# Spectral mixer with MLP, forward and backward on one core: half-row w2-gradient stores on ScalarE's queue, three half rows moved forward, an own tile for x1's gradient

## The chip, the core and the metric

The kernel runs on one core of a Trainium2 chip, in one launch. A core has five engines with an instruction stream each: TensorE (PE, matrix products), VectorE (DVE), ScalarE (ACT), GpSimd (POOL) and SyncE (SP), which here issues loads and stores only. They meet through semaphores. Matrix products land in PSUM, from where DVE or ACT copy them to on-chip memory (SBUF); DMA transfers move data between SBUF and HBM. The metric is the time of one execution in microseconds of device time, the median of several runs.

## The reference

A block with two branches, forward and then the whole backward pass, in bf16 with S = 2048 tokens, D = 1024 channels, F = 3584 hidden channels:

```python
def _A_ref(x, w_r, w_i):          # spectral mixer
    X = rfft2(x, axes=(-2, -1)) * (w_r + 1j * w_i)     # weights 2048 x 513
    return irfft2(X, s=(S, D), axes=(-2, -1)).astype(bfloat16)

def _B_ref(x, w1, b1, w2, b2):    # channel MLP
    y = _layernorm(x)
    h = _gelu(einsum('bsd,df->bsf', y, w1) + b1)       # tanh form
    return einsum('bsf,fd->bsd', h, w2) + b2

mod = (_silu(c) @ w_mod).reshape(c.shape[0], 6, 1, -1)
sa, ca, ga, sb, cb, gb = ...
x = x + ga * _A_ref(_layernorm(x) * (1 + ca) + sa, w_r, w_i)
x = x + gb * _B_ref(_layernorm(x) * (1 + cb) + sb, w1, b1, w2, b2)
```

Outputs are the block's result and the gradients of x, w_r, w_i, w1, b1, w2, b2, c and w_mod. Out of these, this case touches the gradient of w2 (3584 x 1024, `out_6`: h transposed times the gradient at the MLP's output), that of x (`out_1`), and, by their place in the order, those of the spectral weights (`out_2`, `out_3`), of w1 (`out_4`) and of w_mod (`out_9`).

## The kernel before

Work is tiled by P = 128 partitions; a PSUM tile holds 128 x 512 float32 (KH = 512). The forward pass and the MLP's backward come first. The last third of the time, from about 964 us on, runs two things side by side on PE: the backward of the spectral mixer, which is a chain with many hand-overs between engines, and a stock of plain matrix products that depend on nothing in that chain and are dealt out between its steps.

**The stock** is the generator `pieces` (line 1226). It yields first the w2 gradient in half rows: row fc (0 to 27, 128 rows of w2 each) and half h (512 columns) are one product of 16 matmuls of 128x512 (`gw2_product`, 1088, with `gw2_mm`, 1074), which accumulate in a PSUM tile with the tag f (four buffers); `gw2_out` (1078) copies it to SBUF and stores it. The two last rows' four products are interleaved, by token chunks. Then come 56 products of the w1 gradient (line 1266), 16 matmuls each. h comes in by transposing loads (`hh_load`, 1228), and the gradient at the hidden layer by transposing loads too (`gw1_load`, line 1217, tiles gzh), all on SP's queue. `fill(n)` (1277) takes n products.

**The chain** is `spectral_core` (from line 465) in its backward form. It runs eight pairs of frequency blocks: `pair` (495) takes the forward DFT along one axis (matmuls of line 505 into pcs, copied to the tile cs at lines 647 and 650), multiplies on DVE by the weights (tiles Pt, qa, qb, R, all through `tt`, line 173), and makes the gradients of the spectral weights in pf, stored by SP (551) and, by index, by POOL (552). `pair_load` (486) loads weights (490, 491) and the forward's spectrum d_P (493) for the next pair. After each pair `beside_bwd` (1302) takes four products of the stock, with steps of the w_mod gradient between them (`gmod_ring`, 981: load of a strip of w_mod at 986, DVE at 997 and 999, store on POOL at 1000). The inverse DFT `s_inv` (matmuls of line 565 into pv, copied to V by line 647) is done for two classes, CE and SE, ahead of pair 6, and for CO and SO after pair 7. Its pv tiles and half of the pcs and po tiles have the PSUM tag s with two buffers.

Then come four chunks of 512 tokens: matmuls of line 630 into po, copied to ct at 635, and `consume_bwd` (1184), the backward of the layer norm on DVE and ACT, which loads x again (`load_tok`, 128 and 131), adds x1's gradient (`d_gx1`, loaded at 1202 over the normed x) and stores the gradient of x. Between them `fill` takes 6, 6, 8 and 8 products and twice 2 ("norm quarters" are these chunks). After the chunks three more rows of the w_mod gradient follow, with eight products behind each, and the rest of the stock.

**What sets the order.** Each engine runs its own instructions in the order of the program that the scheduler lays down; `high_priority()` lets an instruction go ahead of others that are ready, and `issue_after` ties one to another. A `nc.any` operation is placed by the scheduler on the engine that it thinks free: this goes for the copies of lines 647 (`act_copy`, 646), 635, 1082 and 1270. A DMA from SP or ScalarE takes the next of eight completion semaphores, and waits until the transfer that had this semaphore before has landed; POOL's DMAs have eight of their own. Before the change, ScalarE issues no DMA in this part.

## Time and profile before

| | |
|---|---|
| three runs | 1459.1, 1463.76, 1466.73 us (median 1463.76) |
| the profiled execution | 1459.13 us, of which the span of its instructions 1457.3 |
| granted TensorE clock, mean | 0.992 |
| ACT's waits for a store of the w2 gradient (line 1082), 1000 to 1250 us | 12.6 us, 5 times |
| DVE's waits for the load of x1's gradient (line 173 after 1202) | 3.4 us, 2 times |
| share of the DMA engines, 1080 to 1160 / 1240 to 1360 us | 0.98 / 0.67 to 0.72 |
| last product of the stock ends | 1449.36 us |

In the stretches of 40 us from 1080 on, PE is busy this much (columns: stretch, length, then busy time and instructions of PE, PE's weight loads, DVE, ACT and POOL; then the clock granted to TensorE, the DMA share and GB/s):

```profile
1080.00:1120.00 40.00, 39.94 (x209) 20.22 (x207) 28.51 (x39) 13.22 (x22) 18.03 (x22) 1.00 0.98 249
1120.00:1160.00 40.00, 37.76 (x188) 18.28 (x189) 29.00 (x42) 16.29 (x28) 19.43 (x22) 1.00 0.98 252
1160.00:1200.00 40.00, 38.22 (x188) 18.16 (x187) 26.57 (x38) 14.00 (x25) 17.73 (x21) 1.00 0.85 226
1200.00:1240.00 40.00, 38.88 (x207) 19.43 (x206) 31.95 (x46) 20.00 (x27) 6.93 (x11) 1.00 0.82 223
1240.00:1280.00 40.00, 36.75 (x198) 18.58 (x198) 35.44 (x49) 17.86 (x23) 10.32 (x12) 1.00 0.72 196
1280.00:1320.00 40.00, 39.98 (x207) 19.24 (x205) 34.10 (x45) 17.69 (x23) 11.28 (x16) 1.00 0.69 198
```

How to read it: PE is the engine with the most work in every stretch, and from 1280 us on it never waits; it falls short of 40 us only between 1120 and 1280. That is where pairs 5 to 7, the inverse DFTs and the first chunks lie, and every edit of the change acts there or ahead of it.

### The profile page before, as it was taken

Reading aid. Unit: us, or ns where it says so; the run is one execution under the profiler, and the core shown is the slowest. Engines: PE = TensorE matmul, PEld = TensorE weight load, DVE = VectorE, ACT = ScalarE, POOL = GpSimd, SP = SyncE. Lnnn points to the kernel's source line nnn. Section 1 sums busy time; section 2 is a strip of 40 time slices with the busy share of each in tenths; the row PEclk is TensorE's granted clock in tenths of the full one; section 3 lists DMA queues with packets and bytes.
Section 4 is the critical chain, followed back from the end, with each engine's and each line's share of the span. In section 5 each row is a group of like instructions: output and inputs, shape, how many; then the busy total and the mean of one; then the engine's idle time right before and its main releaser. Section 6 shows DMA issues by size and latency. Waiting matters only on the chain. (4 is left out here: it accounts for less than half of the span.)

```text
span 1457.3 us, 18411 instructions
## 1 busy us (share of the span) xinstructions
PE 1396.5 (96%) x6835; PEld 649.0 (45%) x6835; DVE 1058.4 (73%) x1483; ACT 752.2 (52%) x1065; POOL 366.1 (25%) x441
## 2 busy tenths in 40 slices
PE   5889999999999999999999999999999999999997
PEld 2434545444444444444444444344444445444443
DVE  5884786898799787887520889898467678898650
ACT  4675555857887766665305574342622434344211
POOL 6520451211112122122211011021245441222432
PEclk8999999999999999999999999999999999999999
DMA  9962473899887877697998275297699987766991
GB/s 333 286 214 70 142 235 115 270 255 337 257 203 278 259 250 233 201 264 241 277 297 245 74 271 185 107 270 176 181 217 254 254 233 213 194 191 180 297 279 65
DMA packets 358367, 324.28 MB, mean 223 GB/s; under 512 B 209386, under 2 KB 301056, under 8 KB 358022
## 3 DMA queue, kind: packets, MB, share of 16 engines
q1 hardware_dynamic: 324166, 207.71, 52.7%
q0 software_dynamic: 34112, 115.41, 22.6%
q8 instruction: 53, 0.87, 0.2%
q14 instruction: 36, 0.29, 0.1%
HBM read 162.06 MB, written 111.20 MB: 188 GB/s over the span
## 5 line engine op out<-in xcount | busy, mean ns | idle before, releaser
L684 PE MATMUL pp<-gBoT,wt 128*128 128x512 bf16 x896 | 197.9, 380 | 4.5 <-DMA wt<-in_B_w_dram 2.6
L950 PE MATMUL pg<-w1T,gzr 128*128 128x512 bf16 x896 | 197.1, 381 | 0.2 <-ACT gn3b L961 0.2
L1266 PE MATMUL gw1acc<-gzh,n3n 128*128 128x512 bf16 x896 | 195.4, 379 | 1.3 <-DMA gzh<-d_gz 1.3
L684 PEld LDWEIGHTS <-wt 128*128 128x128 bf16 x896 | 87.7, 98 | 109.4 <-issue 4.2
L950 PEld LDWEIGHTS <-gzr 128*128 128x128 bf16 x896 | 87.3, 98 | 108.7 <-issue 6.6
L802 PEld LDWEIGHTS <-w 128*128 128x128 bf16 x896 | 87.3, 98 | 108.8 <-issue 4.7
L1266 PEld LDWEIGHTS <-n3n 128*128 128x128 bf16 x896 | 87.4, 98 | 106.1 <-issue 2.7
L802 PE MATMUL pz<-n3Tb,w 128*128 128x512 bf16 x448 | 99.2, 379 | 1.6 <-DVE w2sD L875 1.4
L802 PE MATMUL pz<-n3Ta,w 128*128 128x512 bf16 x448 | 98.7, 379 | 1.1 <-ACT gt L805 1.1
L1075 PE MATMUL gw2acc<-gB,hhsA 128*128 128x512 bf16 x448 | 98.5, 379 | 1.0 <-DMA hhsA<-d_hh 1.0
L853 PEld LDWEIGHTS <-hhA 128*128 128x128 bf16 x608 | 59.0, 98 | 71.7 <-issue 1.4
L805 ACT ACTIVATE gt<-pz,b_col 128x512 bf16<-128x512 f32 x112 | 72.5, 684 | 34.2 <-PE pz L802 32.8
L1270 ACT CAST gwo<-gw1acc 128x512 bf16<-128x512 f32 x50 | 29.1, 583 | 113.6 <-PE gw1acc L1266 99.0
L173 DVE TENSOR_TENSOR gt<-gt,gt 128x2048 bf16<-128x2048 bf16 x56 | 68.3, 1223 | 22.4 <-ACT gt L813 21.2
L1082 ACT CAST gwo<-gw2acc 128x512 bf16<-128x512 f32 x46 | 26.7, 583 | 109.9 <-PE gw2acc L1075 75.6
L811 ACT ACTIVATE gt<-gt 128x2048 bf16<-128x2048 bf16 x28 | 53.5, 1910 | 55.7 <-DVE gt L173 55.7
L173 DVE TENSOR_TENSOR ct<-ct 128x2048 bf16<-128x2048 bf16 x64 | 75.9, 1218 | 1.8 <-DMA d_n<-ct 1.1
L1075 PEld LDWEIGHTS <-hhsA 128*128 128x128 bf16 x448 | 43.6, 98 | 53.0 <-DMA hhsA<-d_hh 1.7
L997 DVE CUSTOM_DVE_ANT_0 otl<-otl 128x1024 bf16<-128x1024 bf16 x24 | 29.1, 1223 | 49.9 <-DMA otl<-in_w_mod_dram 44.2
L807 ACT ACTIVATE gt<-gt 128x2048 bf16<-128x2048 bf16 x28 | 53.4, 1908 | 5.4 <-DVE hhC L173 2.5
L813 ACT ACTIVATE gt<-gt 128x2048 bf16<-128x2048 bf16 x28 | 53.5, 1909 | 0.5
L1271 POOL DMA_DIRECT2D out_dram<-gwo x56 | 30.6, 548 | 85.6 <-ACT gwo L1270 53.4
(325 smaller groups left out, 2531.5 us busy)
## 6 DMA issues: line engine op xcount, KB each, us to landing
gzr<-d_gz SPq DMA_DIRECT2D x28, 512.0 KB
wblk<-in_w_mod_dram SPq DMA_DIRECT2D x12, 1024.0 KB
out_dram<-otl POOLq DMA_DIRECT2D x48, 256.0 KB
out_dram<-gwo POOLq DMA_DIRECT2D x96, 128.0 KB
d_ph<-pho POOLq DMA_DIRECT2D x21, 512.0 KB
d_hh<-hhA POOLq DMA_DIRECT2D x19, 512.0 KB
w2sD<-in_B_w_dram SPq DMA_DIRECT2D x14, 512.0 KB
hhC<-d_ph SPq DMA_DIRECT2D x14, 512.0 KB
```

The source lines that it names most:

```text
L173: return nc.vector.tensor_tensor(out=out, in0=a, in1=b, op=op)
L684: last_pe[0] = nc.tensor.matmul(pp[:], lhsT=wt[:, fg % 2, cch, k * P:(k + 1) * P], rhs=gBoT[j][:, cch, :], start=(cch == 0), stop=(cch == ...
L802: last_pe[0] = nc.tensor.matmul(pz[:], lhsT=w1s[g][:, cch, k * P:(k + 1) * P], rhs=n3T[:, cch, :], start=(cch == 0), stop=(cch == NDC - 1))
L805: nc.scalar.activation(out=zb[:, k, :], in_=pz[:], func=ACT.Identity, bias=b1_col[:, fc:fc + 1], scale=1.0)
L807: nc.scalar.activation(out=av, in_=zb, func=ACT.Square)
L811: nc.scalar.activation(out=sg, in_=bv, func=ACT.Sigmoid, scale=2.0 * GK)
L813: nc.scalar.activation(out=bv, in_=bv, func=ACT.Sigmoid, scale=-2.0 * GK)
L853: last_pe[0] = nc.tensor.matmul(pbs[i][:], lhsT=hh[:, k, i * P:(i + 1) * P], rhs=wp[:, k, :], start=False, stop=(g == 6 and k == 3))
L950: last_pg[0] = nc.tensor.matmul(pgs[i][:], lhsT=gzs[b, g][:, k, i * P:(i + 1) * P], rhs=w1Ts[g][:, k, h * KH:(h + 1) * KH], start=(g == 0 ...
L1075: nc.tensor.matmul(acc[:], lhsT=hh_of(fc)[:, t, :], rhs=gBs[t // 4][:, t % 4, h * KH:(h + 1) * KH], start=(t == 0), stop=(t == NT - 1))
L1266: nc.tensor.matmul(acc[:], lhsT=n3ns[t // 4][:, t % 4, cch * P:(cch + 1) * P], rhs=gz2[t // 8][:, t % 8, :], start=(t == 0), stop=(t == NT ...
L1271: nc.gpsimd.dma_start(out=out_4[cch * P:(cch + 1) * P, fg * 512:(fg + 1) * 512], in_=ob)
```

## The change

It has three parts.

1. `gw2_out`: for rows 8 to 27, the PSUM copy stands on ScalarE always, and the half row is stored by ScalarE, at high priority, and not by POOL.
2. `consume_bwd`: x1's gradient gets a tile of its own, gx (four rows of D per partition, tag smb, which smB2 held until the SO inverse), and its load is issued right behind that of x. The addition reads gx.
3. The stock: one product more behind pair 7, 7 and not 6 in the first two chunks; behind each of the last three w_mod rows 7 and not 8.

```diff
     def gw2_out(acc, fc, h):
...
         with tc.high_priority():
-            nc.any.tensor_copy(out=row[:, half], in_=acc[:])
-        if fc >= 8:
-            nc.gpsimd.dma_start(out=out_6[fc * P:(fc + 1) * P, half], in_=row[:, half])
-        elif h == 1:
+            (nc.any.tensor_copy if fc < 8 else nc.scalar.copy)(out=row[:, half], in_=acc[:])
+            if fc >= 8:
+                nc.scalar.dma_start(out=out_6[fc * P:(fc + 1) * P, half], in_=row[:, half])
+        if fc < 8 and h == 1:
             nc.gpsimd.dma_start(out=out_6[fc * P:(fc + 1) * P, :], in_=row)
...
-    accCA = []
+    accCA, gxt = [], []
...
             accCA.append(ps_s("accCA"))
+            gxt.append(reg.tile([P, 4, D], BF16, name="gx", tag="smb"))
...
         load_tok(n1, A_x, i)
+        nc.sync.dma_start(out=gxt[0][:], in_=chunk_rows(d_gx1, i))
         with tc.issue_after(last_po[0].ins):
             norm_act(n1, n1, 0, i)
...
-        nc.sync.dma_start(out=n1, in_=chunk_rows(d_gx1, i))
-        tt(o4, o4, n1, ALU.add)
+        tt(o4, o4, gxt[0][:], ALU.add)
         store_tok(out_1, o4, i)
-        fill((6, 6, 8, 8)[i])
+        fill((7, 7, 8, 8)[i])
...
+        if n == 7:
+            fill(1)
...
         gmod_row(r, w1g["ins"])
-        fill(8)
+        fill(7)
```

## The prediction

> **What bounds the kernel now.** I read the page's busy times, then the waits of TensorE (PE) in the stretch that the change touches (960 us to the end), then the timelines of PE, VectorE (DVE), ScalarE (ACT) and SyncE (SP) around the places where the edits land.

> ```profile
> PE 1396.5 (96%) x6835; PEld 649.0 (45%) x6835; DVE 1058.4 (73%) x1483; ACT 752.2 (52%) x1065; POOL 366.1 (25%) x441
> ```

> PE is busy 96% of the span: the end is set by the sum of its matmuls plus the moments when it waits. Its waits from 960 us on (engine, line, what it waited for: total, times, longest):

> ```profile
> PE po L630 <- ACT ct L635: 2.0, 1, 2.0
> PE pv L565 <- DVE R L173: 1.8, 1, 1.8
> PE gw2acc L1075 <- DMA otl<-d_hh: 1.3, 1, 1.3
> PE gw1acc L1266 <- DMA gzh<-d_gz: 1.3, 1, 1.3
> PE po L630 <- DVE ct L635: 1.1, 1, 1.1
> PE gw2acc L1075 <- DMA hhsA<-d_hh: 1.0, 1, 1.0
> ```

> Six waits, 2.0 + 1.8 + 1.3 + 1.3 + 1.1 + 1.0 = 8.4 us (rounded rows taken from the timeline). That is everything that any change of order can win here: 0.57% of 1459.13. What it can lose has no such bound.

> **The change part by part.** It takes no matmul away and adds none, so the sum is that of PE's waits, old against new. I read the new ones from the order of the changed kernel's instructions and the semaphores they wait for, and their times from rows of before.

> *1. The copy that moves to DVE.* Line 1082's PSUM copies of rows 8 and later are pinned to ScalarE. Line 647's copies (of pv, in the inverse DFT of class CE, just before pair 6) are still free for the scheduler to place. Before, all sixteen before pair 6 stand on ScalarE; in the changed order the first one stands on DVE, behind all of pair 5's arithmetic and two steps of the w_mod gradient (lines 997 and 999, twice). Class CE's pv tiles take turns in two PSUM buffers, so PE's third pv group waits for that copy.

> ```profile
> 1144.89 14.01 PE L565 MATMUL pv<-smi,R 128*128 128x512 bf16 x64
> ```
> ```profile
> 1146.01 0.59 ACT L647 CAST V<-pv 128x512 bf16<-128x512 f32 x1
> ```
> ```profile
> 1143.93 1.28 DVE L173 TENSOR_TENSOR Pt<-cs01b 128x1028 bf16<-128x1028 bf16 x2
> ...
> 1152.48 1.30 DVE L173 TENSOR_TENSOR pf<-qb 128x1026 bf16<-128x1026 bf16 x2
> 1155.63 1.23 DVE L997 CUSTOM_DVE_ANT_0 otl<-otl 128x1024 bf16<-128x1024 bf16 x1 [1.85 <-DMA otl<-in_w_mod_dram]
> ...
> 1159.93 0.49 DVE L999 TENSOR_SCALAR otl<-otl,u_rt 128x1024 bf16<-128x1024 bf16 x1
> ```

> Columns: start, time, engine, line, operation; in brackets the idle time before and what ended it. PE starts the first pv at 1144.89; a group of four matmuls is 14.01 / 16 = 0.87 us, so the third is due at 1146.6. DVE comes to the copy only after 1159.93 + 0.4 = 1160.3, and ends it at about 1161.0 (0.6 us, the ACT row, for want of one on DVE here). PE waits 1161.0 - 1146.6 = 14.4 us. Bounds: without the two waits for w_mod loads (1.85 + 1.27 us) DVE would be there 3.1 us sooner, 11.3; with one of the loads as late as the next one (which cost DVE 7.21 us in place of 1.27), 20.3. I take 14.4, since the loads are the same. What is queued behind the copy on DVE is the w_mod step before pair 6, which waited 7.21 us for its load anyway; behind PE's wait stand the rest of the inverse, pair 6's matmuls and everything after. DVE's pair 6 started at 1169.29 on copies that were there at 1162.0; these come 14.4 later, at 1176.4, so DVE loses only about 7 us of the 14.4 and has caught up with PE by 7.

> *2. ScalarE's stores wait in ScalarE's own order.* All DMAs of SP and ScalarE share eight completion semaphores in rotation, and each waits until the previous holder of its semaphore has landed. Before, SP alone used them. Now 40 half-row stores on ScalarE wait for whatever load of SP came eight DMAs before, and every copy behind them on ScalarE waits too. In pairs 0 to 5 the holders are loads of d_P (493), w_mod (986) and the stores of 551; the copies of pcs queued behind have room of 2.6 to 8 us before DVE wants them (DVE's pair cycle is 16.8 us, PE's 15.6), and gw2acc has four PSUM buffers: I cost them at 0; without that cover it would be the length of each late load, up to 4 us a pair. The last one is bare: the product that is added after pair 7 stores its half row just ahead of seven of CO's copies, and its semaphore's last holder is the third n3n load.

> ```profile
> 1199.71 0.42 SPq L1251 DMA_DIRECT2D n3n<-d_n  x1
> ...
> 1239.43 0.53 SPq L1202 DMA_DIRECT2D xt<-d_gx  x1
> ```

> SP issues it after DVE's pair 7, 6.7 us later than now: 1206.4; a load of that size (d_gx, 1 MB, issued at 1239.43, used at 1246.03) lands 6.6 us on, 1213.0; issue and copy end at 1214.2. PE starts CO's inverse at 1189.86 (its three matmuls ahead of the 1.78 us wait) + 14.4 + 3.46 (the added product of 16 matmuls: half of 1216.03 to 1222.94, the time PE took for two of them at line 1075) = 1207.7 and needs the second buffer back for the fourth group, 2.6 later: 1210.3. Wait 3.9 us; from 0 (the load lands in 2.7 us) to 8. [...]

> *3. One product before CO's inverse* (3.46 us of PE work, moved from the end): it covers the 1.78 us wait for DVE's R, and part 1's shift covers it too: -1.8.

> *4. Two quarters with 7 for 6.* In chunk 1 the extra product brings the gw1 products earlier relative to their first transposed loads. The first product needs the third of SP's transposes:

> ```profile
> 1226.59 12.75 SPq L1217 DMA_TRANSPOSE gzh<-d_gz  x3
> ```
> ```profile
> 1243.34 1.02 PE L1266 MATMUL gw1acc<-gzh,n3n 128*128 128x512 bf16 x4 [1.25 <-DMA gzh<-d_gz]
> ```

> It landed at 1243.3, 20.4 us after the four interleaved last products began (1222.94). In the changed order PE comes to it after these four (13.8 us) and one stretch of other matmuls, 15.6 us after their start: a wait of 4.8 us, from 2 to 6, in place of the 1.1 (line 630, which is now elsewhere) and the 1.3.

> *5. x1's gradient in its own tile.* The load goes out ahead of the norm's arithmetic, and DVE's add no longer waits for it (3.4 us in two waits now). DVE is then through a chunk in some 34.5 us, PE's chunk with nine products (31.1), its po matmuls (3.5) and sums (0.6) is 35.2: PE's 1.98 us wait for line 635 goes, all but 0.5. The tile takes the place of smB2, whose last reader is the SO inverse; the load is queued on SP before the last transposes of hh, and 1 MB there is inside part 4's bound.

> *6. What stays.* The waits for hh (0.96 + 1.34 us) stand on the same order of SP's loads: 2.3. At the end three products fewer run beside and after the w_mod rows; DVE's last step of those (line 977, at 1422.07) ends 26 us before the last product (1449.36), so 26 - 3 x 3.46 = 15.7 us of room is left and nothing waits; the 8 us after the last product stay. POOL loses 40 issues of 0.55 us; at 18 us busy in 40 it was no one's bound: 0.

> Sum of PE's waits after: 2.3 + 14.4 + 3.9 + 4.8 + 0.5 = 25.9; before 8.4: +17.5 us. On the profiled execution (1459.13; span 1457.3 and 1.83 around it) 1476.6. That execution is 4.6 us below the median of the runs (1463.76; 1459.1 to 1466.73), so about 1481 for a median.

> **The rivals.**
> - *DVE comes in time.* DVE's pair 5 had its inputs on chip (the copies of pcs) at 1132; it started at 1143.93 because of a 5.71 us wait for a load in the w_mod step ahead of it and of loads in the pairs before. If taking the 40 stores off POOL's queue loosens that chain of stores and loads, DVE can be up to 11.9 us earlier. The stall of part 1 needs 13.3 us of DVE work after that start (14.4 less 1.1 us of waits that go), so it is gone if pair 5 starts by 1133.3; part 2's load is then earlier as well. PE's waits would be 2.3 + 4.8 + 0.5 = 7.6, 0.8 less than before: 1463; with the transposes in time too, 1458. For it: POOL's share of busy time. Against: line 552's indirect stores on POOL wait for line 551's landing, not for line 1084's issues.
> - *The copy is no stall, but the stores' waits are.* The first V copy is done in time, and ScalarE still blocks before CO's inverse: PE would be at the fourth group at 1195.9, the load, issued at 1199.71, lands between 4.4 (a w_mod load, issued at 1154.25, used at 1158.66) and 6.6 us later, plus 1 us: 9.2 to 11.4 us. With parts 4 to 6, 10 + 7.6 - 8.4 = +9: 1473. Against it: the order, which has the copy behind pair 5.
> - *ScalarE blocks in the pairs as well.* The covers of part 2 are used up once DVE and PE have come level; two or three late loads of 4 us on PE's path: +8 to +12 on top, 1491. For it: the DMA share is 0.98 from 1080 to 1160, so loads are late there. Against it: DVE, the slower one, sets the pace in the pairs.

> **How the numbers follow.** My forecast 0.74, DVE in time 0.08, copy no stall 0.10, blocks in the pairs 0.08. The forecast's own range is 1474 to 1489 (part 1 from 11.3 to 20, part 2 from 0 to 8, part 4 from 2 to 6, not all at one end). The range 1467 to 1491 reaches into the second rival and up to the third and leaves out the first. About 0.5% (7.3 us, the spread of the three runs) can be told from no change: faster 0.03 (of the first rival's), same 0.11 (the rest of it and the half of the second that falls under +7.3), slower 0.86.

> **What would show it.** Right: PE's largest wait in the new profile is pv of line 565 for a DVE copy of line 647, of 11 to 20 us, 1.7 us after CE's inverse starts, with DVE in lines 997 and 999 just before it; a wait of pv for ACT before CO; a wait of the first gw1acc for gzh of 2 to 6 us; the waits for R and for ct of line 635 on ACT gone. Wrong: no wait at line 565 before pair 6, or DVE at pair 5 before 1134; the kernel is then no slower.

## The result, and the profile after

| | before | changed |
|---|---|---|
| median of 6 runs each | 1465.24 us | 1480.16 us |
| lowest to highest | 1458.38 to 1467.34 | 1477.63 to 1484.04 |
| profiled execution (span) | 1459.13 (1457.3) | 1478.41 (1476.6) |
| mean granted TensorE clock | 0.992 | 0.985 |

The changed kernel is slower: ratio 1.0109, 95% interval 1.0089 to 1.013. The profiled executions differ by 19.3 us, the medians by 14.9, since the one profiled before is among that kernel's fastest.

PE's waits from 960 us on, changed kernel (engine, line, what it waited for: total, times, longest; behind line 1203 the new line numbers are one higher):

```profile
PE pv L565 <- DVE V L647: 11.8, 1, 11.8
PE gw1acc L1267 <- DMA gzh<-d_gz: 4.4, 1, 4.4
PE pv L565 <- ACT V L647: 3.6, 1, 3.6
PE gw2acc L1075 <- DMA otl<-d_hh: 2.6, 1, 2.6
PE gw2acc L1075 <- DMA hhsA<-d_hh: 2.2, 1, 2.2
```

Five waits, 24.7 us against 8.4 in six: +16.3. The waits for R, for ct and for po are gone, two for V have come, and those for gzh and hh have grown. The same waits in PE's timeline:

```profile
1139.92 8.77 PE L1075 MATMUL gw2acc<-gB,otl 128*128 128x512 bf16 x32 [2.62 <-DMA otl<-d_hh]
...
1162.20 13.69 PE L565 MATMUL pv<-smi,R 128*128 128x512 bf16 x56 [11.79 <-DVE V L647]
...
1216.77 12.85 PE L565 MATMUL pv<-smB,R 128*128 128x512 bf16 x52 [3.64 <-ACT V L647]
...
1263.58 8.75 PE L1267 MATMUL gw1acc<-gzh,n3n 128*128 128x512 bf16 x32 [4.44 <-DMA gzh<-d_gz]
```

The reader should look at the second column too. 32 matmuls took 7.08 us in the profile of before; here they take 8.77 and 8.75 behind a wait. Counted to the start of what follows, the four stretches lose 1.7, 1.4, 1.5 and 1.7 us, 6.3 together. So the 19.3 us are: 16.3 more of waits, 6.3 of slower matmuls behind them, 3.0 less behind the last product (1471.64 to 1476.6, where it was 1449.36 to 1457.3), and 0.6 that the changed execution was ahead at 963 us, where both programs do the same; that is 19.0, the rest is rounding.

What stood on DVE and ScalarE at the first of these waits (timelines of the two engines):

```profile
1161.06 0.49 DVE L999 TENSOR_SCALAR otl<-otl,u_rt 128x1024 bf16<-128x1024 bf16 x1
1161.46 0.68 DVE L647 CAST V<-pv 128x512 bf16<-128x512 f32 x1
```
```profile
1155.99 0.34 ACTq L1084 DMA_DIRECT2D out_dram<-gwo  x1
1156.38 0.58 ACT L647 CAST V<-pv 128x512 bf16<-128x512 f32 x1 [7.07 <-DMA hhsA<-d_hh]
...
1215.75 0.34 ACTq L1084 DMA_DIRECT2D out_dram<-gwo  x1
1216.13 1.07 ACT L647 CAST V<-pv 128x512 bf16<-128x512 f32 x2 [5.05 <-DMA n3n<-d_n]
```

DVE comes to the first V copy behind the w_mod steps, at 1161.46, as the order said. But ScalarE is late there as well: its half-row store (ACTq, its queue) goes out at 1155.99 only, when a transposing load of h has landed, and the next V copy stands behind it. Before CO it is the same with an n3n load. From this profile alone, DVE's copy could be the whole cause of the first wait or just its last 5 us; the experiments begin there.

### The profile page after: what moved, and what is told of

Read it like the earlier page. It is cut to its first block, busy times and chain, and to the rows that moved or that the text cites. A ratio compares the mean times of both kernels' runs of the same rounds, so it can differ in the third digit from the quotient of the medians.

```text
span 1476.6 us, 18389 instructions
## 1 busy us (share of the span) xinstructions
PE 1405.6 (95%) x6835; PEld 652.3 (44%) x6835; DVE 1061.5 (72%) x1486; ACT 750.5 (51%) x1062; POOL 344.2 (23%) x401
## 5 line engine op out<-in xcount | busy, mean ns | idle before, releaser
L1075 PE MATMUL gw2acc<-gB,hhsA 128*128 128x512 bf16 x448 | 98.3, 379 | 2.2 <-DMA hhsA<-d_hh 2.2
L173 DVE TENSOR_TENSOR gt<-gt,gt 128x2048 bf16<-128x2048 bf16 x56 | 68.4, 1224 | 22.4 <-ACT gt L813 21.2
L173 DVE TENSOR_TENSOR ct<-ct 128x2048 bf16<-128x2048 bf16 x64 | 75.8, 1220 | 1.9 <-DMA d_n<-ct 1.1
L1075 PEld LDWEIGHTS <-hhsA 128*128 128x128 bf16 x448 | 43.8, 98 | 54.0 <-DMA hhsA<-d_hh 2.7
L997 DVE CUSTOM_DVE_ANT_0 otl<-otl 128x1024 bf16<-128x1024 bf16 x24 | 29.1, 1224 | 50.7 <-DMA otl<-in_w_mod_dram 43.8
L647 ACT CAST V<-pv 128x512 bf16<-128x512 f32 x60 | 34.9, 586 | 38.0 <-PE pv L565 25.5
```

Source lines behind the costliest of these rows:

```text
L173: return nc.vector.tensor_tensor(out=out, in0=a, in1=b, op=op)
L647: nc.any.tensor_copy(out=out, in_=in_)
L1075: nc.tensor.matmul(acc[:], lhsT=hh_of(fc)[:, t, :], rhs=gBs[t // 4][:, t % 4, h * KH:(h + 1) * KH], start=(t == 0), stop=(t == NT - 1))
```

## The experiments

Ratios are to the kernel before, run on the same chip with them, with their 95% intervals.

**e1: the V copies pinned to ScalarE.** Everything else as changed.

```diff
-                  new_pair_temps(["t0", "t1", "t2", "t3"]), act_copy, s_copy, act_copy, consume_bwd, "fr", pfs, fill, mid_bwd, beside_bwd)
+                  new_pair_temps(["t0", "t1", "t2", "t3"]), act_copy, s_copy, s_copy, consume_bwd, "fr", pfs, fill, mid_bwd, beside_bwd)
```

> The changed kernel with line 647's V copies (inverse DFT, backward) pinned to ScalarE; stores, tile and fills as changed. Theory A (the copy on DVE is the whole stall): PE's pv wait of 11.8 us before pair 6 goes, and with it the slower matmuls behind it (1.4 us): about 13 us less than the changed kernel, ratio to before about 1.002. Theory B (ScalarE itself stands behind a half-row store that waits for the semaphore of a transposing load of h until 1156.0 in the changed trace, and the DVE copy only covers that): the first V copy ends at about 1156.6, PE waits some 6 us there for ACT instead of 11.8 for DVE; about 5 us less than the changed kernel, ratio about 1.007.

Measured 1477.66 us, ratio 1.0095 (1.0066 to 1.0124): next to nothing. PE's waits and ScalarE's timeline:

```profile
PE pv L565 <- ACT V L650: 14.3, 2, 10.6
```
```profile
1156.12 0.36 ACTq L1084 DMA_DIRECT2D out_dram<-gwo  x1
1156.53 1.07 ACT L650 CAST V<-pv 128x512 bf16<-128x512 f32 x2 [7.66 <-DMA hhsA<-d_hh]
```

Theory B held. The store goes out at 1156.12 (1155.99 with the copy on DVE), and PE waits 10.6 us for ScalarE in place of 11.8 for DVE. The wait expected was 6 us; 3.8 us of the difference is that PE came to the place earlier in this run than in the changed kernel's (1146.6 for 1150.4).

**e2: the half-row stores back on POOL.**

```diff
-            if fc >= 8:
-                nc.scalar.dma_start(out=out_6[...], in_=row[:, half])
-        if fc < 8 and h == 1:
+        if fc >= 8:
+            nc.gpsimd.dma_start(out=out_6[...], in_=row[:, half])
+        elif h == 1:
```

> The changed kernel with the half-row stores of rows 8 to 27 back on POOL (copies pinned to ScalarE, tile gx and fills as changed). Theory: both pv waits (11.8 and 3.6 us) come from the stores on ScalarE's queue, so they go, and the first V copy is placed on ScalarE again; left are the hh waits (2.3 us as before) and the wait of the first w1-gradient product for gzh (4.4 us and 1.7 us of slower matmuls), while the waits for R, for ct and po of before (1.8, 2.0, 1.1) are gone: 1459 us for a profiled execution, ratio 0.998 to 1.002. Rival (the fills or the tile do the harm): ratio 1.006 or more, with pv still waiting.

Measured 1477.85 us, ratio 1.0087 (1.0067 to 1.0108): the rival held. The wait before pair 6 shrank to 1.7 us, but another one took the whole gain, before CO:

```profile
1209.63 14.08 PE L565 MATMUL pv<-smB,R 128*128 128x512 bf16 x56 [11.38 <-ACT V L647]
```
```profile
1193.15 0.59 ACT L1082 CAST gwo<-gw2acc 128x512 bf16<-128x512 f32 x1 [2.87 <-PE gw2acc L1075]
1208.50 0.59 ACT L1082 CAST gwo<-gw2acc 128x512 bf16<-128x512 f32 x1 [14.77 <-DMA out_dram<-gwo]
1208.99 1.08 ACT L647 CAST V<-pv 128x512 bf16<-128x512 f32 x2
```
```profile
1192.77 1.93 POOL L131 DMA_INDIRECT xt<-in_A_x_dram,xu  x1 [0.30 <-issue]
1194.71 1.16 POOL L1084 DMA_DIRECT2D out_dram<-gwo  x2
```

gwo has room for four half rows. The added product's copy is the fifth after pair 7's first, so it needs that one's store to have landed; POOL issued it at 1194.71, behind its indirect loads of x, and ScalarE stood for it from 1193.7 to 1208.5, with the V copies behind. The late issue is not all of it: the copy was done at 1183.4, the store was issued 11.3 us later, and from there to ScalarE's release it took another 13.8 us; what held it on its way was not followed. The fault is in the added product then, on POOL's queue worse (11.4 us) than on ScalarE's (3.6).

**e3, e4 and e10: one part of the change alone.** e3 is the kernel before with the first part (copy and store on ScalarE), e4 with the second (tile gx and the early load), e10 with the third (the fills), each with those lines of the diff and no other.

> The kernel before with the first part alone (copy pinned to ScalarE and half-row store on ScalarE's queue). Theory (stores on ScalarE's queue cost the most): pv waits 11 to 13 us for DVE's V copy before pair 6 with 1.4 us of slower matmuls behind it; before CO there is no store right ahead that waits for an n3n load that late, so 0 to 2 us there; waits for hh, gzh, po and ct as before: 12 to 15 us over before, ratio 1.008 to 1.010. Rival (it takes fills and stores together): ratio under 1.004.

> The kernel before with the second part alone (x1's gradient in the tile gx, loaded early). Theory: DVE no longer waits for that load (3.4 us in two waits before), PE's 2.0 us wait for ct of line 635 goes, the other five waits stay: 2 us less, ratio 0.998 to 1.000. Rival (the early 1 MB load pushes the transposes of h or gzh behind it on SP's queue): the gzh wait grows from 1.3 to 3 us or more, ratio over 1.000.

> The kernel before with the third part alone (one product more behind pair 7, 7 and 7 in the first chunks, 7 behind the last w_mod rows); stores on POOL, no tile gx. Theory (the product ahead of CO makes ScalarE wait for the landing of POOL's store of four half rows ago, behind a w_mod step on POOL's queue, as in e2): pv before CO waits 8 to 12 us for ACT, the first gw1 product 3 to 5 us for gzh: 8 to 14 us over before, ratio 1.006 to 1.009. Rival (in e2 it was the tile's early load that made it late): ratio under 1.003.

| part alone | median | ratio (interval) | largest waits of PE |
|---|---|---|---|
| e3, stores | 1476.14 | 1.007 (1.0038 to 1.0101) | pv for DVE's V 15.2 |
| e4, tile | 1469.41 | 1.0031 (0.9998 to 1.0064) | gzh 3.1, hh 2.3 and 1.5, R 2.3 |
| e10, fills | 1474.89 | 1.0058 (1.003 to 1.0086) | pv for ScalarE's V before CO 12.6, gzh 3.5 |

e3 has the first stall and none before CO, as expected; the wait is longer than the 11 to 13 us expected, the ratio a little under. e4 has the wait for ct down from 2.0 to 0.7 as expected, but gzh at 3.1: its rival's sign, though the interval just holds 1. e10 has e2's stall without the tile, so the fills make it. The three ratios together would be 1.016; in one kernel the parts cost 1.0109. Two likely reasons, not shown one by one, are that the first stall lets DVE and the loads catch up with PE, and that the added product's store on ScalarE is cheaper than on POOL.

**e5: two of the forty stores on POOL.** As e1, and

```diff
-                nc.scalar.dma_start(...)
+                eng = nc.gpsimd if (fc, h) in ((19, 1), (24, 0)) else nc.scalar
+                eng.dma_start(...)
```

> The changed kernel with line 647's backward V copies pinned to ScalarE, and just two of the 40 half-row stores back on POOL: the last one ahead of CE's inverse (row 19, half 1) and the one ahead of CO's (row 24, half 0). Theory (PE's pv waits are the time that ScalarE stands in its own order behind a store whose semaphore belongs to a late load of SP): no store stands ahead of the V copies any more, so both pv waits of e1 (10.6 and 3.7 us) go, with the slower matmuls behind them (1.9 and 1.7): 18 us less than e1, left are hh, and gzh with 5.5 + 2.1: 1458 us, ratio 0.995 to 1.000. Rival (it is the product ahead of CO, whichever queue takes its store, and the copies that wait for the landing of earlier stores, as in e2 with 11.4 us): pv before CO waits 4 us or more for ACT still, ratio over 1.004.

Measured 1470.89 us, ratio 1.0019 (1.0001 to 1.0038), above the 0.995 to 1.000 expected. PE's timeline (line 1268 here is the changed kernel's 1267):

```profile
1151.91 12.25 PE L565 MATMUL pv<-smi,R 128*128 128x512 bf16 x56 [1.86 <-ACT V L650]
...
1205.33 14.62 PE L565 MATMUL pv<-smB,R 128*128 128x512 bf16 x56 [4.66 <-ACT V L650]
...
1255.53 9.94 PE L1268 MATMUL gw1acc<-gzh,n3n 128*128 128x512 bf16 x32 [6.05 <-DMA gzh<-d_gz]
```

Moving one store took the wait before pair 6 from 10.6 to 1.9 us: this is the theory's test, and there it holds. Of the 8.7 us, 3.5 are that PE came later than in e1 (1150.1 for 1146.6); the first V copy began 5.3 us earlier (1151.27 for 1156.53). Before CO the theory did not hold: there the store of row 23 has become the one that waits for an n3n load (ScalarE issued it at 1203.74), and PE arrives 7 us earlier than in e1 (1200.7 for 1207.6).

**e7: the changed kernel without the added product.** The two lines with `if n == 7: fill(1)` taken out.

> The changed kernel without the one product more behind pair 7 (it goes to the end again). Theory: the pv wait before CO is the added product's store; 3.6 us and the 1.5 us of slower matmuls go, and R's wait of before does not return since PE is late by the first stall: 4 to 5 us less than the changed kernel, ratio 1.007 to 1.008; the pv wait for DVE's copy stays at 12 to 15 us. Rival: the store of the product before takes its place, pv before CO still waits 3 us or more for ACT, ratio as the changed kernel's.

Measured 1477.8 us, ratio 1.0088 (1.0059 to 1.0117), which cannot be told from the changed kernel's 1.0109. The wait before CO is gone, as expected, so the cause that the rival names fell, but no 4 to 5 us of the profiled time went with it: gzh has grown from 4.4 to 6.3 us and one wait for hh from 2.2 to 4.6 in the profiled execution, both with slower matmuls behind. That the added product is worth its 5 us is not shown by this run; the wait for hh varies from kernel to kernel anyway (below), and why gzh grew was not followed.

**e6, e8 and e11: gzh in the places that come free first.**

```diff
-        w1g["gz"] = [reg.tile([P, 8, 512], BF16, name=f"gzh{k}", tag=PXT[2 + k]) for k in range(4)]
+        w1g["gz"] = [reg.tile([P, 8, 512], BF16, name=f"gzh{k}", tag=PXT[(3, 4, 2, 5)[k]]) for k in range(4)]
```

The gzh tiles lie where gB was, whose four quarters the interleaved last products give back one after the other; gzh0, needed first, lay in the third. e6 is e5 with this edit, e8 is e4 with it, e11 the changed kernel with it.

> As e5, and the four gzh tiles take the places of gB in the order in which these come free: the two tiles of the first group the places that are free first, not the second and third. Theory (the wait of the first w1-gradient product is for a tile that is loaded third): its first two tiles land two transposes earlier than the last, that wait (5.5 us in e1) goes, with its slower matmuls (1.7): 5 to 7 us less than e5, 1452 us, ratio 0.991 to 0.995. Rival (the transposes as a whole are late, DMA-bound): the wait moves to the second group or stays, within 2 us of e5.

> The kernel before with the second part of the change (tile gx) and the new places of the gzh tiles, nothing else. Theory: e4's gzh wait (3.1 us) goes, and the wait for ct of line 635 stays away; left are hh, R and pv for ACT: 3 us less than e4 and 1 to 3 us less than before, ratio 0.998 to 1.000. Rival (the tile itself does harm): ratio over 1.002.

> The changed kernel with the gzh tiles in the places that come free first, nothing else. Theory: the wait of 4.4 us for gzh and its slower matmuls (1.7) go, everything else stays: 5 to 6 us less than the changed kernel, ratio 1.006 to 1.007. Rival: the wait moves to the second group, ratio 1.009 or more.

e6: 1461.75 us, ratio 0.9972 (0.995 to 0.9994), 9 us less than e5, more than expected; the wait of 6.05 us is gone, and the 2.9 us of slower matmuls behind it went too. e8: ratio 0.9985 (0.9972 to 0.9999), 5 us less than e4, its gzh wait of 3.1 gone. e11: 1473.57 us, ratio 1.0084 (1.0048 to 1.012); the wait of 4.4 is gone from its profile too, but five runs from 1471.74 to 1483.96 do not tell 6 us from 3. For the first product, then, the transposes were not late as a whole; their places were in the wrong order.

**e9: what was learned, put together.** As e6, with the store of row 23, half 1, on POOL as well, and the moved products taken from the chunks: the w_mod rows stand again where they stood before, because in e1, e2, e5 and e6 a late w1 product waited 2.1 to 2.6 us for gzh.

```diff
-                eng = nc.gpsimd if (fc, h) in ((19, 1), (24, 0)) else nc.scalar
+                eng = nc.gpsimd if (fc, h) in ((19, 1), (23, 1), (24, 0)) else nc.scalar
...
-        fill((7, 7, 8, 8)[i])
+        fill((7, 7, 7, 6)[i])
...
-        fill(7)
+        fill(8)
```

> As e6, with three edits: the store of row 23, half 1, on POOL too (in e5 and e6 it became the store that stood before CO's V copies, behind an n3n load); fills of 7, 7, 7 and 6 in the chunks and 8 behind each last w_mod row, so that those rows stand at the same products as before the change (in e1, e2, e5 and e6 a late w1-gradient product waited 2.1 to 2.6 us for gzh there). Theory (each remaining wait is one queue's order): the pv wait before CO (5.5 us) and the late gzh waits (3.2 us) of e6 go, and the slower matmuls behind them (2.4 and 1.8): 8 to 12 us less than e6's profile, ratio to before 0.989 to 0.993. Rival (the product ahead of CO then stands behind the landing of an earlier store, or behind R): pv before CO still waits 3 us or more, ratio 0.995 to 0.999.

Measured 1453.83 us, ratio 0.994 (0.9919 to 0.9961): 0.6% faster than the kernel before and, by the two ratios (0.994 and 1.0109), 1.7% faster than the changed one. All PE waits of its profile from 950 us on, and ScalarE at the place before CO:

```profile
PE gw2acc L1075 <- DMA hhsA<-d_hh: 2.5, 2, 1.7
PE pv L565 <- ACT V L650: 1.9, 1, 1.9
PE po L630 <- DVE ct L635: 1.8, 2, 1.4
```
```profile
1193.51 0.59 ACT L1082 CAST gwo<-gw2acc 128x512 bf16<-128x512 f32 x1 [2.87 <-PE gw2acc L1075]
1194.37 0.59 ACT L650 CAST V<-pv 128x512 bf16<-128x512 f32 x1 [0.28 <-PE pv L565]
```

6.2 us of waits where before had 8.4, none over 2 us, none before CO and none for gzh. Both waits that the theory named went; the ratio is a little over what was expected, with the interval reaching into it. Which of the three edits did how much was not measured apart. And the waits are not the whole gain: this profile's span is 7.1 us shorter than before's (1450.2 for 1457.3), of which 2.2 are waits, 2.2 were won ahead of 964 us, where the two programs do the same, and 2.8 come behind the last product (1445.05 to 1450.2).

## Why the prediction was right, and where it was not

The time (1480.16 for 1481) and the sum of PE's waits (24.7 for 25.9) came out close, but not every reason behind them held, and some of the closeness is luck.

1. *The copy on DVE.* Place and kind were right, 11.8 us for 14.4. DVE was 1.1 us later than put down, PE 3.8: hh waits that were 2.5 us longer, and matmuls slower by 1.7 after one of them. As the cause it was half of the story: e1 moves the copy to ScalarE and wins nothing that can be told. In the changed kernel's trace DVE's copy ends at 1162.14, and ScalarE's next copy, which began at 1156.38, at 1156.96; so 5.2 us of the wait are DVE's alone, and the rest is behind both engines.
2. *ScalarE's stores.* The step that failed is "I cost them at 0" for pairs 0 to 5. The store right ahead of CE's inverse has no cover: the copies behind it are V's, not pcs's. It stood 7.07 us for a transposing load of h, which is not among the holders that the step names. The sharing of the semaphores itself is in the traces' records: before, SP's 447 DMAs take eight in turn and POOL's 386 recorded ones eight others; in the changed kernel SP's 447 and ScalarE's 40 are on the first eight, and 402 and 37 of these have a recorded wait for their own semaphore ahead of the issue. The store issued at 1155.99 has the semaphore of the load of h issued at 1150.15, whose last landing on it is recorded at 1155.92; ScalarE's wait for it ends at 1155.96. With the V copies on ScalarE, this one store makes PE wait nearly as long as behind the DVE copy (10.6 us in e1, 11.8 changed, 1.9 in e5 with the store moved). No run moves that store and leaves the copy on DVE. The store before CO was put down as 3.9 and measured 3.6, but by luck in part: the load that held its semaphore was the second n3n load, not the third; it was issued at 1206.54 (1206.4 put down) and landed 9.1 us later, at 1215.68, not 6.6, and PE came 2.8 us later as well (1213.1 for 1210.3).
3. *The added product.* The wait for R went, as said: in e7 without the product, behind the first stall, and in e9 with the product and without the stall. That POOL's stores could not have borne it (11.4 and 12.6 us in e2 and e10) was not seen; so the parts were not independent.
4. *gzh.* 4.8 put down, 4.4 measured (the tiles landed 20.3 us after the interleaved products began, PE came after 15.8; 20.4 and 15.6 put down), and the cause, the first tile coming third, was right: e6, e8 and e11 take it away by places alone.
5. *The tile.* The 1.98 us went. That it would push gzh (3.1 us in e4, 1.3 before) was put down in step 5 as inside step 4's bound, not as a loss of the tile's own.
6. *What stays.* hh was put down as 2.3 and measured 4.8. This term has no fixed size: over the thirteen profiles, between 1040 and 1300 us, it runs from 0.7 to 6.5, and ahead of 1200 us it differs between kernels that differ only behind that point (before, e4 and e8: 2.3, 5.1 and 4.3). The 8 us behind the last product became 5.0, which was not explained. "Nothing waits" at the end is true of this profile, but four of its relatives waited 2.1 to 2.6 us there (e1, e2, e5 and e6).

Left out altogether: the price of a wait beyond its length, 6.3 us in four stretches. It is offset in part by the shorter end (3.0 us), and the 4.6 us added to come from a profiled execution to a median were 1.8 in the changed kernel: the time agrees by errors of opposite sign, not by precision. The 8.4 us of waits were also called all that a change of order can win; e9's shorter end shows that they are not.

The first rival (DVE in time) fell: DVE began pair 5 at 1145.99. The second, ScalarE's stores as the wait, was true beside the forecast and not in place of it. The third, stores that block in the pairs, was true of ScalarE, which stood up to 9.2 us there (for a w_mod load, to 1140.9), but PE waited for no copy of it before CE's inverse.

## What to carry to other kernels

Here a store issued from ScalarE waited in that engine's own order, and what it waited for was a load on SP's queue that had nothing to do with it (7.07 us for a load of h): before moving stores, find the load that held each store's semaphore and the instruction standing behind the store. Move single stores, not all: three of forty back on POOL, with the V copies pinned, four tiles in other places and the fills dealt anew, made 0.6% faster of 1.1% slower. Where a stall has an obvious culprit, take only that away and look whether the next engine is late by as much.

## What the runs showed of the hardware

A wait of PE cost more than its length here: 1.4 us on top of the 11.79 before pair 6, 1.7 on top of the 4.44 for gzh. The clock granted in the 3.4 us after two waits of the changed kernel (stretch, length, busy times and instructions of PE, PEld, DVE, ACT and POOL, then clock, DMA share, GB/s):

```profile
1162.20:1165.60 3.40, 3.40 (x10) 1.24 (x10) 0.00 (x0) 0.62 (x2) 0.21 (x1) 0.57 0.73 233
...
1263.60:1267.00 3.40, 3.40 (x10) 1.32 (x11) 1.71 (x1) 0.00 (x0) 0.00 (x0) 0.58 1.26 291
```

10 matmuls in 3.4 us where the kernel before ran 16 (1192.5 to 1195.9, behind a wait of 1.78 us, clock 1.00). From 950 us on, over all thirteen profiles, a wait of up to 2.1 us before a long stretch of matmuls lost 0.4 us at most; of eleven between 2.1 and 2.4 us, seven lost 1.3 to 1.8 and four 0.2 at most; from 2.5 us on each lost 1.4 to 2.9, where enough matmuls followed to measure it.

```profile
1137.83:1141.24 3.41, 1.32 (x7) 0.62 (x8) 0.00 (x0) 0.34 (x1) 0.00 (x0) 1.00 1.02 238
1141.25:1144.65 3.40, 3.40 (x10) 1.17 (x9) 1.83 (x3) 0.82 (x2) 2.00 (x2) 0.50 1.11 197
...
1117.35:1120.76 3.41, 2.00 (x10) 0.69 (x7) 0.15 (x1) 0.00 (x0) 0.00 (x0) 1.00 1.16 167
1120.77:1124.17 3.40, 2.60 (x12) 1.19 (x13) 2.14 (x4) 0.42 (x1) 0.23 (x1) 1.00 1.15 311
1124.18:1127.58 3.40, 3.40 (x17) 1.56 (x16) 3.33 (x6) 0.74 (x2) 3.09 (x3) 1.00 0.64 197
```

PE was idle for 2.1 us of the first window, and the next one ran at half clock. The other wait was cut in two, 1.4 and 0.8 us, and cost nothing. Over all thirteen profiles, from 100 us on, no window at full clock with up to 1.95 us of idle time was followed by one at half clock, and all 46 with 2.03 us or more were; the two between went one each way (1.96 fell, 2.01 did not).

By an estimate from these records, 3.41 us at a clock of 0.50 lose 1.7 us; the four stretches of the changed kernel lost 1.4 to 1.7.
